# Two attention blocks on one core: the late tiles of A projected in pairs for each load of weights, with the loads of weights and of k moved to other steps

## The chip, the core and the metric

The kernel runs on one core of a Trainium2 chip. Its engines are TensorE (PE, with PEld for its weight loads), VectorE (DVE), ScalarE (ACT), GpSimd (POOL) and SyncE (SP), whose queue issues nearly all DMAs here. The metric is the device time of one execution in microseconds, less being better; a version's time is the median of several executions.

## What is computed

Two independent multi-head attentions over 2048 rows of 640 numbers in fp32, 32 heads of 20, each with its own input and weights. A is local and dilated (each row looks at eight rows, two apart, backwards), B is full attention. The outputs stand side by side.

```python
def _A_ref(x, wqkv, wo):          # H = 32, Dh = 20, W, dil = 8, 2
    qkv = (x @ wqkv).reshape(B, S, 3, H, Dh)   # then split into q, k, v
    idx = pos[:, None] - (jnp.arange(W) * dil)[None, :]
    kg, vg = k[:, :, idx_c, :], v[:, :, idx_c, :]
    logits = jnp.where(mask, jnp.einsum("bhsd,bhswd->bhsw", q, kg) * scale, -1e9)
    o = jnp.einsum("bhsw,bhswd->bhsd", softmax(logits), vg)
    return o.reshape(B, S, D) @ wo

def _B_ref(x, wqkv, wo):
    scores = jnp.einsum("bhqd,bhkd->bhqk", q, k) * (Dh ** -0.5)
    o = jnp.einsum("bhqk,bhkd->bhqd", softmax(scores), v)
    return o.reshape(B, S, D) @ wo

jnp.concatenate([a, b], axis=-1)
```

## The kernel before

**Numbers.** fp32 operands of the projections are split into a high and a low part, and three products of them (`PASSES`) stand for one fp32 product: high by high, high by low, low by high. The scores of B use the same trick within one matmul: a head's stack of q and k holds high and low rows together (`BS` = 60 rows, `BM` = 62 with two more that carry the maximum of the row).

**Stages.** First the projections: A's tiles 0 to 11 of 128 rows (the loop over `NA` parts of the weights, with the split weights kept in DRAM in `wa_d` by `a_keep`), then B's q and k (the loop over `m`), then B's v in 32 groups (`v_group`, the stage of V groups). The attention of A itself is elementwise work on POOL (`a_attention`: 4 steps of scores and 4 of values for each tile, with k and v rows fetched from `ka_d` and `va_d` into the tile `akv`), and runs beside everything else.

**The loop.** From about 397 us on, a loop of 514 steps does B's attention: 8 groups of four heads (g), 4 blocks of 512 queries (qc), 16 blocks of 128 keys (kb). Sixteen steps are a unit: one group with one query block. There are 32 units, numbered 0 to 31 here; unit 4g is the first of group g, so the first units of groups are even ones. In each step the scores of one key block are made and their exponential taken (ACT `e`), the row maxima of a unit 24 steps ahead are found (DVE `mx`), and an earlier block of exponentials is multiplied with v (`b_pv`, into an accumulator in PSUM). `UNIT_V` and `UNIT` write out the order of these on PE by hand; `b_units` plays it. A `V` in the list, near the start of each of units 0 to 23, is one call of `a_more`: it projects one of A's late tiles (12 to 15) by one of six parts m of A's weights (320 columns), 15 matmuls with the tile `wx`, in all 4 tiles by 6 parts.

**The end of a unit.** For every second key block ACT copies the accumulator out: the first copy of a unit goes to a tile `braw` (of which there are two), the later seven to tiles `more`, and POOL adds those to `braw`. At the unit's last block `normalize` starts a chain that lies in the next unit: the sums of the rows leave for DRAM (`s_d<-braw`), come back with another layout (`sm<-s_d`), DVE takes their reciprocals at the place marked `G`, these go out (`s_d<-sm`) and return spread over partitions (`rb<-s_d`), POOL multiplies `braw` by them, and four DMAs store the result (`ot_b<-braw`). The `braw` of unit u is thus free again only when its four stores have been made, in unit u+1; the first copy of unit u+2 goes to the same tile. That copy is the unit border that the text uses: "unit 10" begins when ACT starts the copy to its `braw`.

**Loads that the change touches.**

- `a_load` allocates `wx` (one buffer, shared with an earlier tile) and loads the weights of the next call in two DMAs of 800 KB (high and low part). It is called 10 steps after each `V`, and its DMAs are issued one and two steps later: 24 loads, one for each `V`.
- `b_keys(g + 1)` loads the next group's stack of k (tile `bk`) in four DMAs, two of 40 rows and two of 22. It runs at step 4 of a group; the DMAs follow 1, 2, 17 and 18 steps later, that is in steps 5 and 6 of unit 4g and in steps 5 and 6 of unit 4g+1.
- `a_columns(t)` loads the columns of A's input for tile t (320 KB) and splits them on POOL five steps later (4 operations); it runs in the stage of V groups for tile 12 and after the last `V` of a tile for the next one.
- `v_piece` loads rows of B's v for a group.

**What sets the order.** `after(n, fn)` puts a call n steps later; each engine runs its instructions in the order in which the program emits them, SP's DMA issues included. A DMA whose tile is still read, or whose source is not yet written, holds back every DMA behind it on SP. In odd units the finished tile of A is turned as well: `tr_d<-turn` and four `back<-tr_d` move 320 KB out and back.

All work on tiles goes through one line of the class `InOrder`, so the profile gives line 61 to almost everything; the tiles tell the groups apart.

Of the kernel before, what the change touches and what calls it, by code (L numbers as in the profile page):

```python
# [9 lines left out]
F32 = mybir.dt.float32  # L10
# [31 lines left out]
UP = 12  # L42
# [23 lines left out]
def attention_pair(ctx, tc, xa, wqk_a, wv_a, wo_a, xb, wqk_b, wv_b, wo_b, oa, ob):  # L66
# [6 lines left out]
    pe, gp, sp = (InOrder(tc, e) for e in (nc.tensor, nc.gpsimd, nc.sync))  # L73
# [6 lines left out]
    def after(n, fn, *args):  # L80
        due.setdefault(now[0] + n, []).append((fn, args))
# [22 lines left out]
    def tick():  # L104
        now[0] += 1
        for fn, args in due.pop(now[0], ()):
            fn(*args)
# [58 lines left out]
    wa_d = dr.tile([6, 128, 2, KC, 320], F32, name="wa_d")  # L166
# [22 lines left out]
    def big(home, shape, name):  # L189

        return sb.tile(shape, F32R, tag=f"big{home}", bufs=1, name=name)
# [6 lines left out]
    def chunk(t, xi, k):  # L198
        return t[k // (KC - 1)][:, xi, k % (KC - 1)]

    def x_pieces(x, n, second=None, at=()):

        t = columns(*at or (n,))
        src = x[:, n * 512:(n + 1) * 512].rearrange("(k p) c -> p k c", p=128)

        def piece(a, b):
            u = t[a // (KC - 1)]
            m = a % (KC - 1)
            split(u[:, 0, m:m + b - a], u[:, 1, m:m + b - a], src[:, a:b], "p", second)
        return t, [lambda a=a, b=b: piece(a, b) for a, b in PAIRS]  # L210
# [10 lines left out]
    AK = ((0, 3), (3, KC))  # L221
# [94 lines left out]
    t, more = x_pieces(xa, 1, at=(2,))  # L316
# [5 lines left out]
    t, loads = x_pieces(xa, 2, at=(3,))  # L322
# [218 lines left out]
    for n in range(NA):  # L541
        nxt = None
        for t in range(UP):
# [19 lines left out]
            if n == 1 and t == 7:  # L563
                w, more = x_pieces(xb, 0)
                XB.append(w)
                loads += more
            if n == NA - 1:
                if t in (1, 2):
                    w, more = m_pieces(MS[t - 1])
                    WB.append(w)  # L570
                    more[0]()
                if t % 4 == 0 and t:
                    w, more = x_pieces(xb, t // 4)
# [5 lines left out]
    w, loads = x_pieces(xb, 3)  # L579
# [21 lines left out]
    def v_piece(g, b0, b1):  # L601

        sp.dma_start(stacks[g][1][:, b0:b1], vb_d[b0 * 128:b1 * 128, g * GH * VC:g * GH * VC + VG]
                     .rearrange("(b p) c -> p b c", p=128))
# [7 lines left out]
    groups = 0  # L612
    for m in range(0, 10, 2):
        nxt = []
        for n in range(4):
            for j in range(2):
# [14 lines left out]
                if m < 8 and (n, j) in ((1, 0), (1, 1)):  # L631
                    w, loads = m_pieces(MS[m + 2 + len(nxt)])
# [317 lines left out]
    groups = 0  # L950

    def v_group(n, half, s):
        p = bank()
        rows15(p, lambda xi, k: chunk(XB[n], xi, k)[:, s % 4 * 128:s % 4 * 128 + 128], WV[half])
        ve = ones[s % 4]
        act.copy(ve[:, :16 * VC].rearrange("p (h c) -> p h c", c=VC)[:, :, :DH],
                 p[:, :320].rearrange("p (h d) -> p h d", d=DH))
        give(p)
        c = 16 * VC + 11 * half
        after(1, sp.dma_start, vb_d[s * 128:(s + 1) * 128, half * 16 * VC:half * 16 * VC + c], ve[:, :c])  # L960
# [7 lines left out]
            W.append(w)  # L968
            loads.extend(more)

    rows_a = [(t, m) for t in range(UP, NT) for m in range(6)]
    xt, wt = [], []
    in_dram = [UP]

    def a_columns(t):

        u = sb.tile([128, 640], F32, tag="stg", bufs=3, name="stg")
        raw = u.rearrange("p (k c) -> p k c", c=128)
        sp.dma_start(raw, xa[:, t * 128:(t + 1) * 128].rearrange("(k p) c -> p k c", p=128))
        x = (sb.tile([128, 2, KC - 1, 128], F32R, tag="last1", bufs=2, name="xn"),  # L980
             sb.tile([128, 2, 1, 128], F32R, tag="x5", bufs=2, name="xl"))

        def parts():
            for u, r in zip(x, (raw[:, :KC - 1], raw[:, KC - 1:])):
                gp.tensor_copy(u[:, 0], r)
                gp.tensor_tensor(u[:, 1], r, u[:, 0].bitcast(F32), ALU.subtract)
            xt.append(x)
        after(5, parts)

    def a_load():  # L990

        if not rows_a:
            return
        t, m = rows_a[0]
        w = big(2, [128, 2, KC, 320], "wx")
        for wi in range(2):
            after(1 + wi, sp.dma_start, w[:, wi].bitcast(F32), wa_d[m, :, wi])
        wt.append(w)

    def a_more():  # L1000

        t, m = rows_a.pop(0)
        if m == 0 and len(xt) > 1:
            xt.pop(0)
        x, w = xt[0], wt.pop(0)
        p = bank()
        rows15(p, lambda xi, k: chunk(x, xi, k), [w[:, 0], w[:, 1]])
        hf, r0 = divmod(t * 128, HS)
        pad = PAD if m > 1 else 0
        store_rows(p, (qa_d, ka_d, va_d)[m // 2][hf, pad + r0:pad + r0 + 128, m % 2 * 320:m % 2 * 320 + 320])  # L1010
        if m == 5:
            after(2, in_dram.__setitem__, 0, t + 1)
            if rows_a:
                after(2, a_columns, t + 1)
        after(10, a_load)

    V_GROUPS = [(n, half, s) for n in (2, 3, 0, 1) for half in range(2) for s in range(4 * n, 4 * n + 4)]
    v_late = V_GROUPS[-LAG:]
    for n, half, s in V_GROUPS[:-LAG]:
        v_group(n, half, s)  # L1020
        tick()
        groups += 1
        if q_loads:
            for _ in range(4 if groups == 1 else 1):
                q_loads.pop(0)()
        if groups == 1:
            wait[0] = 5
        if groups in (8, 16):
            XB[groups // 8 - 1], more = x_pieces(xb, groups // 8 - 1, gp, (groups // 8 - 1, groups // 8 + 1))
            for fn in more:  # L1030
                fn()
        if groups > 6:
            for i in islice(steps, 1):
                b_max(i)
        if groups in (9, 11, 15, 17, 19, 23, 25, 28):
            next(a_work, None)
        if groups in (26, 28):
            v_piece(0, *((0, 4) if groups == 26 else (8, 16)))
        if groups in (24, 28):
            (a_load if groups == 28 else lambda: a_columns(UP))()  # L1040
        if groups == 14:
            a_turn(*done_a.pop(0)[1:])
        turn_parts()
        if groups == 28:
            wait[0] = 2
            load_out(wo_a, WO, (0,))
        if loads and groups >= 28:
            loads.pop(0)()
# [22 lines left out]
    def flush():  # L1071
        while beside:
            op = beside.pop(0)
            (small if len(op) > 1 else op[0])(*(op if len(op) > 1 else ()))
# [9 lines left out]
    for i in range(NS + LAG):  # L1084
        g, sub = divmod(i, NQC * NKB)
        if sub == 4 and g + 1 < NG:
            for n, fn in enumerate(b_keys(g + 1)):
                after((1, 2, 17, 18)[n], fn)
            after(33, v_piece, g + 1, 0, NKB)
        if i >= NKB and i % NKB in (1, 3, 5, 7) and i // NKB + 3 < NG * NQC:  # L1090
            b_queries(*divmod(i // NKB + 3, NQC))[i % NKB // 2]()
        if i in (NS - 56, NS - 40):
            out_first((i - NS + 56) // NKB)
        tick()
        if loads and i % 2:
            loads.pop(0)()
        if i > 14 and i % 4 == 3 and next(a_work, 0) == 0:
            for d in done_a:
                d[0] -= 1
        if i % NKB == SLOT and done_a and done_a[0][0] <= 0:  # L1100
            beside.append((lambda d=done_a.pop(0): a_turn(*d[1:]),))
        turn_parts()
        if i == 1:
            load_out(wo_a, WO, (1,))

            spare += [sb.tile([128, 2, 512], F32, tag="last0", bufs=2, name="more") for _ in range(2)]
        if i < NS - LEAD:
            next(steps, None)
            if not left_a[0] and not WO_b:
                load_out(wo_b, WO_b)  # L1110
            continue
        read_at.clear()
        flush()
        if i < NS:
            b_qk(i)
        if i % 2:
            b_pv(i - LAG - 1)
            b_pv(i - LAG)
            if fill:
                fill.pop(0)()  # L1120
# [57 lines left out]
```

## Time and profile before

| what | value |
|---|---|
| time, median of 3 runs (lowest to highest) | 1801.79 us (1799.25 to 1805.84) |
| the profiled execution: its own time, and the span of its instructions | 1804.91 us, 1803.1 us |
| PE busy | 1766.3 us, 98% |
| DVE, ACT, POOL busy | 1345.8 us (75%), 1333.3 us (74%), 1230.8 us (68%) |
| DMA traffic | 289.41 MB, 161 GB/s on average |
| stage of projections of A, and of q and k of B | 0 to 318 us |
| stage of V groups | 318 to 397 us |
| units 0 to 23 of the loop (with a `V` each) | 400.57 to 1431.48 us |
| the rest of the loop and the output projection of B | 1431.48 us to the end |

The span runs from the first to the last instruction; the execution's own time is 1.8 us more. A row of a group reads: line, engine, operation, out<-in by the program's names, sizes, count, then the time busy. In a view of waits each row is "who waited <- for whom: us in total, times, longest". In a timeline each row is start, duration, engine, operation, tiles, count, and in brackets how long the engine sat idle before it and what ended that. SPq rows are issues of DMAs by SP, not the transfers. The windows view gives, for a stretch, its length, each engine's busy time (and count of instructions), then the granted share of the TensorE clock, the mean busy share of the 16 DMA engines, and GB/s.

### The profile page before, as it was taken

Reading aid. Unit: us, or ns where it says so; the run is one execution under the profiler, and the core shown is the slowest. Engines: PE = TensorE matmul, PEld = TensorE weight load, DVE = VectorE, ACT = ScalarE, POOL = GpSimd, SP = SyncE. Lnnn points to the kernel's source line nnn. Section 1 sums busy time; section 2 is a strip of 40 time slices with the busy share of each in tenths; the row PEclk is TensorE's granted clock in tenths of the full one; section 3 lists DMA queues with packets and bytes.
Section 4 is the critical chain, followed back from the end, with each engine's and each line's share of the span. In section 5 each row is a group of like instructions: output and inputs, shape, how many; then the busy total and the mean of one; then the engine's idle time right before and its main releaser. Section 6 shows DMA issues by size and latency. Waiting matters only on the chain.

```text
span 1803.1 us, 32021 instructions
## 1 busy us (share of the span) xinstructions
PE 1766.3 (98%) x11331; PEld 1010.4 (56%) x11331; DVE 1345.8 (75%) x1819; ACT 1333.3 (74%) x2598; POOL 1230.8 (68%) x1088
## 2 busy tenths in 40 slices
PE   9999999999999999999999999999999999999999
PEld 7988888774444445444444444444544444444569
DVE  3102232779899989998999899989889999999400
ACT  4323222239799989998989898888889999989981
POOL 0000782686788888897989798979787988845532
PEclk9999999999999999999999999999999999999999
DMA  7657877865545553555465546554554534222223
GB/s 255 192 178 247 296 255 244 243 201 144 154 148 154 170 163 125 173 152 165 155 167 164 181 136 188 161 161 139 169 164 143 139 111 123 80 69 66 63 70 113
DMA packets 212137, 289.41 MB, mean 161 GB/s; under 512 B 91660, under 2 KB 131724, under 8 KB 210984
## 3 DMA queue, kind: packets, MB, share of 16 engines
q1 hardware_dynamic: 211400, 286.70, 52.0%
q8 instruction: 89, 1.46, 0.3%
q14 instruction: 72, 0.59, 0.1%
q10 hardware_dynamic: 576, 0.66, 0.1%
HBM read 212.53 MB, written 74.74 MB: 159 GB/s over the span
## 4 chain that ended last, share of the span: by engine, by line
PE 85%; DVE 6%; DMA 6%; ACT 1%; issue 1%; SPq 0%; POOL 0%; ACTq 0%; DVEq 0%
PE ps_st L61 85%; DVE mx L61 6%; DMA ot_b<-braw 3%; DMA wx<-wa_d 2%; ACT e L61 1%; DMA bq<-qb_d 1%; DMA stg<-wv_b 0%; ACT braw L61 0%; DMA stg<-xa 0%; SPq L61 0%; DMA qb_d<-pr 0%; POOL am L61 0%; DVE xl L61 0%; ACTq L61 0%; DVE pr L61 0%
## 5 line engine op out<-in xcount | busy, mean ns | idle before, releaser
L61 DVE TENSOR_REDUCE mx<-ps_st 128x1 f32<-128x512 f32 (+1 forms) x1500 | 1220.0, 878 | 116.1 <-PE ps_st L61 105.9
L61 ACT ACTIVATE e<-ps_st 128x512 f32<-128x512 f32 x2048 | 1067.2, 608 | 38.2 <-PE ps_st L61 19.1
L61 PE MATMUL ps_st<-bq,bk 62*128 62x512 f32 x2048 | 611.9, 442 | 0.8 <-DVE mx L61 0.6
L61 PE MATMUL ps_st<-bk,bq 60*128 60x512 f32 x2048 | 559.0, 434 | 26.0 <-ACT braw L61 23.7
L61 PEld LDWEIGHTS ps_st<-bq,bk 62*128 62x128 f32 x2048 | 289.7, 185 | 479.8 <-ACT e L61 352.9
L61 PE MATMUL ps_st<-e,vb 128*32 128x512 f32 x4096 | 542.9, 604 | 3.2 <-ACT e L61 0.3
L61 POOL TENSOR_TENSOR braw<-braw,more 128x512 f32<-128x512 f32 x224 | 288.2, 1287 | 220.7 <-ACT more L61 200.4
L61 POOL TENSOR_TENSOR akv<-akv,aq 128x1280 f32<-128x1280 f32 x64 | 188.6, 2947 | 184.4 <-DVE w L61 184.4
L61 PEld LDWEIGHTS ps_st<-bk,bq 60*128 60x128 f32 x2048 | 270.5, 185 | 60.9 <-ACT braw L61 27.2
L61 POOL TENSOR_TENSOR akv<-akv 128x640 f32<-128x640 f32 (+3 forms) x304 | 282.9, 930 | 23.8
L61 ACT COPY ro<-ps_st 128x320 f32<-128x320 f32 (+2 forms) x132 | 62.5, 475 | 201.6 <-PE ps_st L61 169.0
L61 PEld LDWEIGHTS ps_st<-e,vb 128*32 128x32 f32 x4096 | 82.0, 108 | 158.6 <-issue 72.0
L61 POOL TENSOR_TENSOR akv<-akv,al 128x1280 f32<-128x1280 f32 x64 | 152.1, 2377 | 0.2
L61 ACT COPY more<-ps_st 128x512 f32<-128x512 f32 x224 | 132.5, 592 | 1.9 <-PE ps_st L61 1.4
L61 PE MATMUL ps_st<-ww,xn 128*128 128x320 f32 x768 | 125.8, 314 | 0.0
L61 PEld LDWEIGHTS ps_st<-ww,xn 128*128 128x128 f32 x768 | 113.6, 188 | 19.9 <-ACT e L61 8.4
L61 PE MATMUL ps_st<-xn,w 128*128 128x512 f32 x480 | 117.6, 393 | 0.0
L61 PEld LDWEIGHTS ps_st<-xn,w 128*128 128x128 f32 x480 | 90.1, 188 | 21.0
L61 PE MATMUL ps_st<-wc,xn 128*128 128x512 f32 (+1 forms) x432 | 101.5, 380 | 0.1
L61 ACT CAST pr<-ps_st 128x512 fp32r<-128x512 f32 x40 | 23.5, 589 | 103.5 <-PE ps_st L61 103.5
L61 DVE TENSOR_TENSOR pr<-ps_st,pr 128x512 fp32r<-128x512 f32 x40 | 27.7, 691 | 92.9 <-ACT pr L61 90.1
L61 PEld LDWEIGHTS ps_st<-wc,xn 128*128 128x128 f32 x432 | 79.9, 188 | 14.5 <-ACT xn L61 0.8
(69 smaller groups left out, 1083.8 us busy)
## 6 DMA issues: line engine op xcount, KB each, us to landing
akv<-ka_d SPq DMA_DIRECT2D x128, 320.0 KB
akv<-va_d SPq DMA_DIRECT2D x128, 320.0 KB
wx<-wa_d SPq DMA_DIRECT2D x48, 800.0 KB
kb_d<-pr SPq DMA_DIRECT2D x20, 512.0 KB
qb_d<-pr SPq DMA_DIRECT2D x20, 512.0 KB
bk<-kb_d SPq DMA_DIRECT2D x16, 640.0 KB
bq<-qb_d SPq DMA_DIRECT2D x64, 160.0 KB
rb<-s_d SPq DMA_DIRECT2D x128, 64.0 KB
```

Source lines behind the costliest of these rows:

```text
L61: return self.tc.keep_in_program_order(op(*a, **k))
```

## The change

Four edits:

1. The 24 calls of `a_more` run in another order: tiles 12 and 13 take turns on each part m, then 14 and 15. One load of `wx` serves two calls, so there are 12 loads in place of 24. A load is issued in four DMAs (the 3 and 2 chunks of rows `AK` of the high part, then of the low part; 480 and 320 KB), 2 to 5 steps after the second of the two calls, which lands in steps 5 to 8 of odd units. The first load moves from V groups 29 and 30 to groups 25 to 28.
2. The four DMAs of the next k stack go in steps 5 to 8 of unit 4g, all of them.
3. The columns of tiles 12 and 13 are both loaded in the stage of V groups (after groups 18 and 21), those of 14 and 15 twelve steps after the last call of tile 12 and of tile 13 (units 10 and 11).
4. In the stage of V groups two pieces of v (`v_piece`, blocks 8 to 16) are loaded earlier, after groups 22 and 23 in place of 28.

```diff
-    rows_a = [(t, m) for t in range(UP, NT) for m in range(6)]
-    xt, wt = [], []
+    rows_a = [(t + j, m) for t in range(UP, NT, 2) for m in range(6) for j in range(2)]
+    xt, wt = {}, []
...
     def a_load():
 
-        if not rows_a:
-            return
-        t, m = rows_a[0]
         w = big(2, [128, 2, KC, 320], "wx")
-        for wi in range(2):
-            after(1 + wi, sp.dma_start, w[:, wi].bitcast(F32), wa_d[m, :, wi])
-        wt.append(w)
+        wt[:] = [w]
+        m = rows_a[0][1]
+        return [lambda wi=wi, a=a, b=b: sp.dma_start(w[:, wi, a:b].bitcast(F32), wa_d[m, :, wi, a:b])
+                for wi in range(2) for a, b in AK]
 
     def a_more():
 
         t, m = rows_a.pop(0)
-        if m == 0 and len(xt) > 1:
-            xt.pop(0)
-        x, w = xt[0], wt.pop(0)
+        x, w = xt[t], wt[0]
...
         if m == 5:
             after(2, in_dram.__setitem__, 0, t + 1)
-            if rows_a:
-                after(2, a_columns, t + 1)
-        after(10, a_load)
+            if t + 2 < NT:
+                after(12, a_columns, t + 2)
+        if t % 2 and rows_a:
+            for n, fn in enumerate(a_load()):
+                after(2 + n, fn)
...
-        if groups in (26, 28):
-            v_piece(0, *((0, 4) if groups == 26 else (8, 16)))
-        if groups in (24, 28):
-            (a_load if groups == 28 else lambda: a_columns(UP))()
+        if groups in (22, 23, 26):
+            v_piece(0, *((8, 12), (12, 16), (0, 4))[(groups - 21) // 2])
+        if groups in (18, 21):
+            a_columns(UP + groups // 21)
+        if groups == 24:
+            for n, fn in enumerate(a_load()):
+                after(1 + n, fn)
...
             for n, fn in enumerate(b_keys(g + 1)):
-                after((1, 2, 17, 18)[n], fn)
+                after(1 + n, fn)
```

PE, ACT and DVE run the same operations in the same order as before; SP and POOL do not. On SP, in the second half of an odd unit (unit 3), where the turned tile comes back and `braw` is stored, these rows stand before the change:

```order
L61 DMA back<-tr_d 32x20x32 x4
L61 DMA wx<-wa_d 128x1600 x2
L61 DMA akv<-va_d 128x640 x2
L61 DMA bq<-qb_d 20x1024
L61 DMA ot_b<-braw 20x512 x4
L61 DMA bq<-qb_d 40x1024
```

And the same place after it:

```order
L61 DMA back<-tr_d 32x20x32 x4
L61 DMA akv<-va_d 128x640 x2
L61 DMA bq<-qb_d 20x1024
L61 DMA ot_b<-braw 20x512 x4
L61 DMA bq<-qb_d 40x1024
```

The two loads of `wx` ahead of the four stores of `braw` are gone there, and in the even units too. In the first half of the same odd unit SP has now, between the return of the sums and the store of their reciprocals:

```order
L61 DMA sm<-s_d 128x16
L61 DMA wx<-wa_d 128x960
L61 DMA wx<-wa_d 128x640
L61 DMA bq<-qb_d 40x1024
L61 DMA wx<-wa_d 128x960
L61 DMA akv<-va_d 128x640 x2
L61 DMA wx<-wa_d 128x640
L61 DMA oa<-ro 128x320
L61 DMA s_d<-sm 128x16
```

All four pieces stand behind `sm<-s_d` and ahead of `oa<-ro`, the first DMA of the second half. In unit 4, the first of a group, SP has before the change:

```order
L61 DMA bk<-kb_d 40x4096
L61 DMA bq<-qb_d 20x1024
L61 DMA sm<-s_d 128x16
L61 DMA bk<-kb_d 22x4096
L61 DMA bq<-qb_d 40x1024
L61 DMA aq<-qa_d 128x640
L61 DMA akv<-ka_d 128x640 x2
```

And after it:

```order
L61 DMA bk<-kb_d 40x4096
L61 DMA bq<-qb_d 20x1024
L61 DMA sm<-s_d 128x16
L61 DMA bk<-kb_d 22x4096
L61 DMA bk<-kb_d 40x4096
L61 DMA bq<-qb_d 40x1024
L61 DMA bk<-kb_d 22x4096
L61 DMA aq<-qa_d 128x640
L61 DMA akv<-ka_d 128x640 x2
```

The second half of the k stack has come here from steps 5 and 6 of the next unit by the program's count of steps, which SP had issued at the end of this unit and the start of the next.

More of the change, by code (lines that the diff above doesn't have):

```diff
@@ L986, in parts @@
                 gp.tensor_tensor(u[:, 1], r, u[:, 0].bitcast(F32), ALU.subtract)
-            xt.append(x)
+            xt[t] = x
         after(5, parts)
     def a_load():
-        if not rows_a:
-            return
-        t, m = rows_a[0]
         w = big(2, [128, 2, KC, 320], "wx")
-        for wi in range(2):
-            after(1 + wi, sp.dma_start, w[:, wi].bitcast(F32), wa_d[m, :, wi])
-        wt.append(w)
+        wt[:] = [w]
+        m = rows_a[0][1]
+        return [lambda wi=wi, a=a, b=b: sp.dma_start(w[:, wi, a:b].bitcast(F32), wa_d[m, :, wi, a:b])
+                for wi in range(2) for a, b in AK]
     def a_more():
         t, m = rows_a.pop(0)
-        if m == 0 and len(xt) > 1:
-            xt.pop(0)
-        x, w = xt[0], wt.pop(0)
+        x, w = xt[t], wt[0]
         p = bank()
```

## Prediction

> **What bounds the kernel now.** I read the page first, then the waits of each engine within the loop, then the timeline around the longest of them, then windows over single units.
>
> ```profile
> span 1803.1 us, 32021 instructions
> PE 85%; DVE 6%; DMA 6%; ACT 1%; issue 1%; SPq 0%; POOL 0%; ACTq 0%; DVEq 0%
> core 0: 1803.1 us, clock 0.991
> ```
>
> The chain that ended last is PE for 85% of the span; 6% of it runs over DMAs. Where does PE wait in the loop? The waits from 397 to 1700 us, ACT's own three and PE's largest:
>
> ```profile
> ACT braw L61 <- DMA ot_b<-braw: 24.8, 8, 4.1
> ACT braw L61 <- PE ps_st L61: 1.7, 2, 0.9
> ACT braw L61 <- DVE mx L61: 1.7, 1, 1.7
> PE ps_st L61 <- ACT braw L61: 23.7, 11, 3.7
> ```
>
> PE has one wait worth the name, on ACT's copy to `braw`: 11 times, 23.7 us. ACT in turn waits 8 times for the stores of the `braw` of two units ago, 24.8 us, the longest 4.1. The other three (1.7 and 1.7 us) I put to the same cause, since the same copy waits for the same semaphores and the view names only the last one. So 28.2 us of waits on one tile. One of the eight, from unit 9 to unit 10, on SP:
>
> ```profile
> 790.04 0.34 SPq L61 DMA_DIRECT2D sm<-s_d  x1
> 790.84 0.82 SPq L61 DMA_DIRECT2D akv<-va_d  x2
> ...
> 805.52 0.47 SPq L61 DMA_DIRECT2D s_d<-sm  x1
> ...
> 814.95 2.69 SPq L61 DMA_DIRECT2D back<-tr_d  x4
> 817.74 1.29 SPq L61 DMA_DIRECT2D wx<-wa_d  x2
> 819.09 1.12 SPq L61 DMA_DIRECT2D akv<-va_d  x2
> ...
> 820.76 2.11 SPq L61 DMA_DIRECT2D ot_b<-braw  x4
> ```
>
> and on POOL, ACT and PE:
>
> ```profile
> 813.19 1.29 POOL L61 TENSOR_TENSOR braw<-braw,rb 128x512 f32<-128x512 f32 x1
> 828.72 0.59 ACT L61 COPY braw<-ps_st 128x512 f32<-128x512 f32 x1 [2.98 <-DMA ot_b<-braw]
> 829.35 0.50 PE L61 MATMUL ps_st<-bk,bq 60*128 60x512 f32 x1 [2.58 <-ACT braw L61]
> ```
>
> `braw` is ready at 814.5 (813.19 + 1.29), but its stores are issued from 820.76 on, behind `back`, the two `wx` loads of 800 KB and an `akv`, and they land just before 828.7. ACT stands 2.98 us, PE 2.58. What a unit costs with and without this, in windows from copy to copy (units 0 to 23 together, then 7, 8, 9, 10 and 23):
>
> ```profile
> 400.57:1431.48 1030.91, 1002.55 (x6866) 483.17 (x6867) 949.48 (x1307) 913.05 (x1789) 856.62 (x753) 0.99 0.52 156
> 701.26:743.25 41.99, 41.88 (x293) 20.19 (x293) 40.70 (x59) 37.98 (x76) 38.46 (x34) 1.00 0.45 138
> 743.25:784.62 41.37, 40.68 (x282) 19.23 (x283) 38.40 (x52) 38.15 (x75) 33.18 (x30) 1.00 0.60 185
> 784.62:828.72 44.10, 42.04 (x293) 20.18 (x293) 42.67 (x61) 37.95 (x76) 40.47 (x36) 1.00 0.55 153
> 828.72:871.45 42.73, 41.90 (x281) 20.53 (x283) 36.53 (x49) 38.14 (x75) 31.15 (x28) 0.96 0.51 164
> 1389.96:1431.48 41.52, 41.39 (x288) 19.49 (x289) 39.80 (x58) 37.98 (x75) 38.03 (x34) 1.00 0.40 111
> ```
>
> Unit 9 ends with the wait: 44.10 − 2.98 = 41.12 without it. Unit 10 has none, yet takes 42.73 where unit 8 takes 41.37: the last columns but two show why, its granted clock is 0.96. A wait of this length costs a second time, 1.36 us, as a spell of lower clock just after it. In unit 10 the spell is (1 − 0.96) × 42.73 × 2 = 3.4 us at half clock, and the mean clock of 0.991 over the span is 0.009 × 1803.1 × 2 = 32 us at half, nine such spells, near the eight long waits. The Trainium skill, "TensorE: Matmul & The Clock Gate", section "HAM oscillation — how this bites in real kernels", has the rule that a gap of PE beyond some 3.4 us drops it to half clock and that half of the throttled time is lost. The trace shows the drop after 2.58 us already, and the price per spell is 1.36 us by rows, 1.7 by the page; over 32 us that would be 12.8 or 16 us.
>
> **The change part by part.**
>
> *The loads of weights leave the end of the units.* Traffic first, from the list of DMA issues and from windows:
>
> ```profile
> wx<-wa_d SPq DMA_DIRECT2D x48, 800.0 KB
> bk<-kb_d SPq DMA_DIRECT2D x16, 640.0 KB
> 790.60:797.00 6.40, 6.40 (x48) 2.69 (x47) 6.40 (x8) 6.18 (x13) 4.39 (x4) 1.00 0.90 176
> 797.00:805.00 8.00, 7.93 (x57) 4.83 (x53) 7.67 (x18) 7.23 (x15) 7.39 (x11) 1.00 0.03 11
> 814.00:828.70 14.70, 12.77 (x91) 5.08 (x89) 14.40 (x18) 11.42 (x23) 14.39 (x11) 1.00 0.91 285
> 747.80:756.00 8.20, 8.17 (x61) 3.42 (x60) 8.06 (x11) 7.99 (x17) 4.15 (x3) 1.00 0.83 197
> 756.00:764.30 8.30, 8.14 (x57) 4.74 (x54) 7.32 (x13) 7.46 (x15) 6.44 (x8) 1.00 0.34 99
> ```
>
> In the last 14.7 us of unit 9 the DMA engines are 91% busy at 285 GB/s; from 797 to 805 they are 3% busy. The change takes 1.64 MB out of the first stretch, 1.64 MB / 285 GB/s = 5.7 us of its work, and 1.29 us of SP's issuing, and half of all such loads vanish. What the stores gain is bounded by 1.3 us (the issue alone) below and 5.7 us above. I take the upper end, for two reasons. The waits of SP from 784 to 829 us say that its later issues hang on the loads too:
>
> ```profile
> SPq L61 <- DMA wx<-wa_d: 2.6, 2, 1.8
> SPq L61 <- DMA s_d<-sm: 2.8, 1, 2.8
> ```
>
> (2.6 us that go, whereas the 2.8 us for the reciprocals stay). And unit 23 is already what an odd unit will be: it has `back`, `akv` and the stores, but no load of weights behind its `V`:
>
> ```profile
> 1418.72 2.70 SPq L61 DMA_DIRECT2D back<-tr_d  x4
> ...
> 1424.03 1.44 SPq L61 DMA_DIRECT2D ot_b<-braw  x4
> ```
>
> Its stores are issued 34.1 us after its start (unit 9: 36.1), all four within 1.44 us (unit 9: 2.11), and the copy at 1431.48 starts without idle time. A gain of 5.7 us covers the longest wait of 4.1.
>
> The sum, two ways. By waits: 28.2 us, and 9.4 spells × 1.36 = 12.8; together 41.0. By units: if all 24 ran like unit 8, 24 × 41.37 = 992.9 against 1030.91, 38.0 us. Unit 23 (41.52) is a little above that, unit 9 without its wait (41.12) a little below. I take **38.0**, which leaves room for small waits under 1 us like that at the end of unit 7; 41 stays as the end of the range below.
>
> *The loads in steps 5 to 8 of odd units.* The four pieces follow `sm<-s_d` (790.04 in unit 9). With the `akv` of 0.66 MB that is 2.3 MB from about 791; at 176 to 285 GB/s it ends at 799 to 804, inside the idle stretch and ahead of `s_d<-sm` at 805.52. What is queued behind them on SP: `bq`, which is for a unit three later, `akv`, and then nothing for 14 us. The `akv` issued at 790.84 is used here:
>
> ```profile
> 815.68 2.37 POOL L61 TENSOR_TENSOR akv<-akv,al 128x1280 f32<-128x1280 f32 x1
> ```
>
> 24.8 us later, so 8 us of delay cost nothing. The next `V` reads the weights a unit later. Cost 0; if that cover were gone, POOL would be late by what `akv` is late, and `braw` with it.
>
> *The k stack in one piece.* The first halves of the stack in unit 8 and what follows:
>
> ```profile
> 747.76 0.31 SPq L61 DMA_DIRECT2D bk<-kb_d  x1
> ...
> 764.21 0.38 SPq L61 DMA_DIRECT2D s_d<-sm  x1
> ...
> 777.19 1.45 SPq L61 DMA_DIRECT2D ot_b<-braw  x4
> ```
>
> The 756 to 764 window is 34% busy: the second half (0.99 MB, 5.0 us at the 197 GB/s beside it) fits, and ends about when `s_d<-sm` starts. If it overlaps, the reciprocals come up to 2 us later, in a unit that has no `back`, loses 5.7 us of weights and had no wait at its end. Cost 0, bounds −1 (the start of unit 4g+1 is freed) to +2 us once per group.
>
> *Columns and v.* The columns of tiles 14 and 15 (320 KB, 1.1 us at 285 GB/s) now stand ahead of the stores in units 10 and 11, and those of two other units go; POOL's four operations each are as many as before. Bounds −2 to +2 us; I take 0. In the stage of V groups the loads come some four groups earlier, and PE's waits there are on no DMA; 0, with up to 4 us (one wait of 2.6 and its spell) if a store of v is held back.
>
> Sum for the profiled execution: 1804.9 − 38.0 = 1766.9. It stands 3.1 us above the median of the runs, so for a median I predict 1801.8 − 38.0 = **1764 us**.
>
> **The rivals.**
>
> *Only the issue is saved.* `back` and `akv` stay ahead of the stores, and the transfers may be so spread over the DMA engines that the stores land only 1.3 us earlier. Then 24.8 − 8 × 1.3 = 14.4 us of waits stay with most spells; gained are 10.4 + 3.4 = 13.8, which gives 1788. For it: unit 9's reciprocals came back 2.8 us late and that stays. Against: unit 23. Chance 0.10.
>
> *It does not do what it says:* `back` alone decides, the weights only filled time in which the stores waited anyway, and nothing that can be measured moves: 1799. Against it stands the same unit, and that even units, without `back`, show no wait at all speaks for it. Chance 0.07.
>
> *A new wait, and slower.* DVE takes the reciprocals of the sums in its fixed place:
>
> ```profile
> 803.36 0.20 DVE L61 RECIPROCAL sm<-sm 128x16 f32<-128x16 f32 x1
> DVE sm L61 <- DMA sm<-s_d: 14.1, 2, 7.1
> ```
>
> In unit 9 that is 13.3 us after `sm<-s_d` was issued; at the end of the kernel DVE did wait for it twice, 7.1 us at most. In the first unit of a group it stands behind 640 KB of k with 1.4 MB following. If the small transfer landed later than those 13 us, DVE and then PE would stand: 7 groups × (7.1 + 1.36) = 59 us, and 1764 + 59 = 1823. Against: a whole half stack and its neighbours were done by about 760, 12 us after issue, with the small one ahead of half of it. Chance 0.06.
>
> **How the numbers follow.** Forecast 0.77, the rivals 0.10, 0.07 and 0.06. The forecast's own range is 1764 − 3 (the sum by waits) − 4 (the bounds of the k stack, the columns, and a run's scatter) to 1764 + 8 (the upper bounds of stack, columns and V groups), 1757 to 1772. To hold the time 8 times in 10 it takes in half of the first rival: 1756 to 1783. A measurement of this kernel tells 0.5%, 9 us, from no change. Faster by more: forecast and first rival, 0.87; within: 0.07; slower: 0.06.
>
> **What would show it.** Right: ACT's waits for `ot_b<-braw` gone or under 3 us in all, clock 1.00 in the windows of all units, units 0 to 23 in some 993 us, DMA busy in the first half of odd units and below 70% in the last 14 us. Wrong: waits of 2 us or more left at the ends of units 1, 5, 9 and so on (first rival), ACT's wait unchanged (second), DVE waiting for `sm<-s_d` within the loop (third), or PE waiting on `wx`.

## The result, and the profile after

| | median of the runs (lowest to highest) | profiled execution | clock |
|---|---|---|---|
| before | 1800.52 us (1798.07 to 1805.84, 4 runs) | 1804.91 us | 0.991 |
| after | 1771.25 us (1770.04 to 1776.2, 4 runs) | 1771.62 us | 0.999 |

The ratio is 0.9839, with a 95% interval of 0.9809 to 0.9868: the change saves 29.3 us by the medians and 33.3 us between the two profiled executions. The forecast was 1764 us; the time is 7.3 us above it, within the range. First the page of the kernel after: its span, the chain that ended last, and its DMA packets.

```profile
span 1769.8 us, 31997 instructions
PE 85%; DMA 4%; DVE 4%; POOL 3%; issue 1%; SPq 1%; ACT 1%; DVEq 0%; POOLq 0%; ACTq 0%
DMA packets 212152, 269.74 MB, mean 152 GB/s; under 512 B 91676, under 2 KB 131740, under 8 KB 211000
```

DMA's share of the chain has gone from 6% to 4%, and the traffic from 289.41 to 269.74 MB, which are the twelve loads of 1.64 MB that pairing saves. The waits in units 0 to 23 (400 to 1398 us), first ACT's largest, then PE's largest:

```profile
ACT ro L61 <- PE ps_st L61: 53.1, 48, 1.6
...
PE ps_st L61 <- DMA bq<-mdr: 3.9, 5, 1.1
```

No row of ACT's copy to `braw` is left, where there were 28.2 us, and PE no longer waits for that copy. In its place stands a row that the kernel before did not have: PE waits five times for the rows with the maxima (`bq<-mdr`). The windows from copy to copy say what the two are worth: units 0 to 23 together, then units 4, 6 and 9, then the last 14.2 us of unit 9.

```profile
403.34:1397.50 994.16, 985.55 (x6866) 470.15 (x6867) 948.93 (x1307) 912.76 (x1789) 854.38 (x750) 1.00 0.49 142
568.25:610.74 42.49, 41.15 (x288) 19.46 (x290) 39.38 (x53) 38.18 (x76) 32.92 (x27) 1.00 0.55 149
651.83:693.20 41.37, 41.13 (x288) 19.69 (x290) 39.25 (x53) 38.16 (x76) 34.01 (x30) 1.00 0.40 121
776.15:817.27 41.12, 41.01 (x288) 19.67 (x289) 39.84 (x58) 37.93 (x75) 38.70 (x37) 1.00 0.51 150
803.10:817.30 14.20, 14.20 (x104) 5.68 (x104) 14.04 (x19) 13.88 (x28) 13.96 (x12) 1.00 0.74 211
```

Units 0 to 23 take 994.16 us, 36.7 less than before, at a clock of 1.00. Odd units (41.12) and most even ones (41.37) run as the wait-free units of before did. Unit 4, the first of a group, takes 42.49. In unit 9 the end is busy still, 74% of the DMA engines at 211 GB/s (before: 91% at 285). What SP issues in unit 9, and the copy that ends it:

```profile
781.49 0.85 SPq L61 DMA_DIRECT2D wx<-wa_d  x2
...
806.60 2.70 SPq L61 DMA_DIRECT2D back<-tr_d  x4
809.34 1.12 SPq L61 DMA_DIRECT2D akv<-va_d  x2
...
811.30 1.40 SPq L61 DMA_DIRECT2D ot_b<-braw  x4
...
817.27 0.59 ACT L61 COPY braw<-ps_st 128x512 f32<-128x512 f32 x1
```

The stores are issued 35.2 us after the start of the unit (before: 820.76 − 784.62 = 36.1). The issue has come only 1 us earlier, and still the copy, which stood 2.98 us before, has no idle time in front of it. The rest lies between issue and transfer. In the packets of the traces (2 KB each, one row of a store) the first row follows the issue by 4.9 us before and by 1.7 after, and the last one ends 43.1 and 39.2 us after the start of the unit. What the stores gained is the 1.6 MB that no longer go ahead of them.

**Where 33.3 us come from.** Units 0 to 23: −36.7. The first copy to `braw` comes at 403.34 in place of 400.57: +2.8. The rest of the span, 1803.1 − 1431.48 = 371.6 before and 1769.8 − 1397.5 = 372.3 after: +0.7, which is within what this stretch varies by in the other profiles (371.5 to 372.4). So something went wrong in two places, and both are one kind of wait.

*The k stack.* Unit 4 on SP, then POOL's product and PE's wait:

```profile
572.76 0.31 SPq L61 DMA_DIRECT2D bk<-kb_d  x1
...
573.95 1.05 SPq L61 DMA_DIRECT2D bk<-kb_d  x2
575.66 0.35 SPq L61 DMA_DIRECT2D bk<-kb_d  x1
...
589.20 0.38 SPq L61 DMA_DIRECT2D s_d<-sm  x1
...
594.76 2.15 SPq L61 DMA_DIRECT2D rb<-s_d  x4
597.03 1.74 SPq L61 DMA_DIRECT2D mdr<-mtr  x4
...
600.13 0.56 SPq L61 DMA_DIRECT2D bq<-mdr  x2
```

```profile
598.64 1.28 POOL L61 TENSOR_TENSOR braw<-braw,rb 128x512 f32<-128x512 f32 x1 [2.68 <-DMA rb<-s_d]
603.02 0.50 PE L61 MATMUL ps_st<-bq,bk 62*128 62x512 f32 x1 [1.10 <-DMA bq<-mdr]
```

The 8 KB of reciprocals (`s_d<-sm`) are issued at 589.20, 20.9 us into the unit, and `rb<-s_d`, which must wait for their landing, only at 594.76, 5.6 us later (in units 4 and 8 of the kernel before it came some 1.5 us later). SP stands in between, and what stands behind it on SP is `mdr<-mtr` and `bq<-mdr`, which have nothing to do with the reciprocals: they bring the maxima for the next scores on PE. Why the 8 KB landed late is seen in the DMA view's row of busy shares. Its 40 slices run from 744 to 765 us of the kernel before (unit 8) and from 572 to 592 us of the kernel after (unit 4):

```profile
DMA  8200000099163896969997977766662000000007
```

```profile
DMA  0069125687676985956999988662789586247566
```

Before, the DMA engines fall idle at about 760, five microseconds ahead of the next store. After, they are busy right to the end of the stretch, and `s_d<-sm` goes out into it.

*The stage of V groups.* ACT and PE after:

```profile
386.78 0.43 ACT L61 COPY ve<-ps_st 128x320 f32<-128x320 f32 x1 [3.57 <-DMA vb_d<-ve]
390.71 0.42 ACT L61 COPY ve<-ps_st 128x320 f32<-128x320 f32 x1 [3.50 <-DMA vb_d<-ve]
391.40 0.46 PE L61 MATMUL ps_st<-bq,bk 62*128 62x512 f32 x1 [1.92 <-DMA bq<-mdr]
```

Before, PE's longest idle time between 380 and 402 us was 0.86. Now the first load of weights and two pieces of v stand there ahead of small DMAs, and PE waits 1.92 us. (ACT is idle some 2.6 us before most copies of this stage in any case, waiting for PE, so about 0.9 us of each of its two waits is new.) The only spell of lower clock of this execution, but for its last 1.4 us, follows: 3.41 us at half from 392.89 on.

### The profile page after: what moved, and what is told of

It is laid out like the page before. It is cut to its first block, busy times and chain, and to the rows that moved or that the text cites. A ratio compares the mean times of both kernels' runs of the same rounds, so it can differ in the third digit from the quotient of the medians.

```text
span 1769.8 us, 31997 instructions
## 1 busy us (share of the span) xinstructions
PE 1751.3 (99%) x11331; PEld 999.9 (56%) x11331; DVE 1345.4 (76%) x1819; ACT 1333.0 (75%) x2598; POOL 1230.0 (70%) x1088
## 2 busy tenths in 40 slices
DMA packets 212152, 269.74 MB, mean 152 GB/s; under 512 B 91676, under 2 KB 131740, under 8 KB 211000
## 4 chain that ended last, share of the span: by engine, by line
PE 85%; DMA 4%; DVE 4%; POOL 3%; issue 1%; SPq 1%; ACT 1%; DVEq 0%; POOLq 0%; ACTq 0%
PE ps_st L61 85%; DVE mx L61 4%; DMA s_d<-sm 1%; POOL akv L61 1%; SPq L61 1%; DMA bq<-mdr 1%; ACT e L61 1%; DMA bq<-qb_d 1%; POOL xn L61 0%; DMA stg<-wv_b 0%; DMA mdr<-mtr 0%; DMA wx<-wa_d 0%; DMA qb_d<-pr 0%; POOL xl L61 0%; POOL ao L61 0%
## 5 line engine op out<-in xcount | busy, mean ns | idle before, releaser
L61 PEld LDWEIGHTS ps_st<-xn,w 128*128 128x128 f32 x480 | 90.2, 188 | 20.9
L61 ACT CAST pr<-ps_st 128x512 fp32r<-128x512 f32 x40 | 23.5, 587 | 103.6 <-PE ps_st L61 103.6
```

Of the source, the lines that this page charges most:

```text
L61: return self.tc.keep_in_program_order(op(*a, **k))
```

## The experiments

**Theories.** (P) *Place*: the bytes of the weights ahead of the four stores at the end of the odd units made all the waits; moving them is the whole gain. (T) *Traffic*: half the loads is what counts, wherever they lie. (I) *Issue*: SP's time for the two DMAs counts, not the bytes. For the 4 to 6 us given back: (K) the k stack in one piece, and (F) the early first load in the stage of V groups.

### Place and traffic apart

Place alone: the kernel before, with all 24 loads, each in the four pieces right after its `V`.

```diff
-        for wi in range(2):
-            after(1 + wi, sp.dma_start, w[:, wi].bitcast(F32), wa_d[m, :, wi])
+        for n, (wi, (a, b)) in enumerate((wi, ab) for wi in range(2) for ab in AK):
+            after(lag + n, sp.dma_start, w[:, wi, a:b].bitcast(F32), wa_d[m, :, wi, a:b])
...
-        after(10, a_load)
+        a_load()
```

> The kernel before, with one thing of the change: each of its 24 loads of weights goes in four pieces 2 to 5 steps after its call, in steps 5 to 8 of every unit. No pairs, k and the stage of V groups as before. Theory (the place ahead of the stores of braw is what cost the time): ACT waits for ot_b<-braw under 3 us in all, no spell of lower clock, units 0 to 23 in 990 to 997 us, time 1762 to 1770. Rival (half the traffic is what counts): the traffic is that of before, so the waits stay above 12 us and the time above 1785. Second rival (two loads in steps 5 to 8 of a group's first unit, weights and k together, jam there): waits on bq<-mdr in units 4, 8, 12 and so on.

Pairs alone: the kernel after with 12 loads, each of two DMAs and in the old place; the k stack, the first load and the pieces of v as before, too.

```diff
-            for n, fn in enumerate(a_load()):
-                after(2 + n, fn)
+            after(10, a_load)
...
-                after(1 + n, fn)
+                after((1, 2, 17, 18)[n], fn)
```

> The changed kernel with its loads of weights back where they were in odd units: two pieces of 800 KB, 11 and 12 steps after the second call of a pair; k in steps 5, 6, 21, 22 as before; first load and v pieces in the stage of V groups as before, but both columns early (after groups 18 and 21). Half of the traffic of the weights, none of the new places. Theory (place): the eight long waits all follow odd units, and these keep their loads, so ACT's waits for ot_b<-braw stay at 20 to 28 us and the time at 1790 to 1803. Rival (traffic): waits fall to about half, 10 to 14 us, time 1783 to 1789. For the stage of V groups: if the early columns on POOL are what made PE wait 1.92 us for bq<-mdr at 391 us, the first copy to braw stays at 403 us; if the early weights are, it comes at 400.5 to 401.

| | median (lowest to highest) | ratio to before (95%) |
|---|---|---|
| place alone | 1765.45 us (1765.22 to 1766.17) | 0.9809 (0.9783 to 0.9835) |
| pairs alone | 1800.34 us (1797.11 to 1803.82) | 1.0004 (0.9989 to 1.002) |

Units 0 to 23 in place alone, in the windows view (PE's only wait from 397 to 1440 us is one of 0.3):

```profile
400.98:1391.98 991.00, 986.23 (x6866) 471.24 (x6866) 948.70 (x1307) 913.04 (x1790) 856.53 (x753) 1.00 0.57 163
```

and in pairs alone, the window, ACT's waits on the copy and PE's:

```profile
403.11:1428.16 1025.05, 1001.60 (x6866) 482.37 (x6866) 949.33 (x1307) 912.89 (x1790) 854.87 (x752) 0.99 0.48 138
```

```profile
ACT braw L61 <- DMA ot_b<-braw: 18.9, 8, 3.5
ACT braw L61 <- POOL akv L61: 2.8, 1, 2.8
ACT braw L61 <- DVE mx L61: 1.1, 1, 1.1
ACT braw L61 <- PE ps_st L61: 0.7, 1, 0.7
...
PE ps_st L61 <- ACT braw L61: 19.0, 11, 3.0
```

Place alone moves 163 GB/s in these units, more than any kernel here without added copies, and has no wait on the copy. Pairs alone moves 138 and keeps 23.5 of the 28.2 us. The place is the whole gain; halving the traffic is worth nothing in this kernel, since the twelve loads that it saves lay in units that had no wait at their end. (Nor is it worth anything where no wait is left: pairs at the new place, with the stack of k and the first load put back, take 1765.84 us below.) And place alone is 5.8 us faster than the change (6.2 us when both ran again on one chip, at 1767.19, 1765.44 to 1768.35, and 1773.35, 1771.27 to 1778.07, with no overlap):

> place_alone once more beside the changed kernel. If the place is the whole gain and the rest of the change costs: 1765 to 1767, 4 to 7 us below changed_again. If chips differ by as much: within 2 us of it.

> The changed kernel itself, on the same chip as the others of this call. If its new waits (k stack, stage of V groups) are a matter of place and not of the execution: again 1770 to 1774, five waits on bq<-mdr in the first units of groups, and one on bq<-mdr before the first copy to braw.

One reading of pairs alone misled: its first copy to `braw` is as late as in the kernel after (403.11), which looks like the loss in the stage of V groups. It isn't. PE's wait for `bq<-mdr` is gone there, and what is late is the start of the stage, by a wait of 1.51 us on `bq<-qb_d` at 318.02 (before: 0.51 at 316.95) and a spell of lower clock right behind it. The time of one event sums all that lies before it; the stage by itself, from the ninth V group's copy to the first copy to `braw`, takes 76.4 us in pairs alone, 76.5 before and 78.6 after.

### Bytes or issue: a dose at the old place

Place alone plus copies of a part of `wa_d` into a DRAM tile that nothing reads, issued where the loads of the odd units stood. Nothing that is computed changes; the copies are added work. The doses are two DMAs of 1.3 KB (the issue only), 480 + 320 KB, and 2 × 800 KB.

```diff
+    def again(m):
+        for wi, part in enumerate(((slice(0, 128), slice(0, 3)), (slice(0, 128), slice(0, 2)))):
+            after(1 + wi, sp.dma_start, junk[wi, part[0], part[1]], wa_d[m, part[0], wi, part[1]])
...
         a_load()
+        calls[0] += 1
+        if calls[0] % 2 == 0:
+            after(10, again, m)
```

> place_alone with two DMAs of 1.3 KB each added in odd units where the loads stood before (11 and 12 steps after the V): SP's two issues without the bytes. It prices the lower bound of the prediction. Theory (bytes ahead of the stores cost the time): no waits on ot_b<-braw above 1 us in all, 1765 to 1767. Rival (SP's issuing and the order of its queue cost it): waits of 8 us or more in all, 1773 or above.

> As dose_issue, with 480 and 320 KB copied within DRAM in place of the small ones: half the bytes of the old loads. Theory: the stores land some 2.9 us later; the margin at the ends of the odd units after a group's first unit is 5.7 less 3.1 to 4.1 us, so only these six show waits, of about 1 us, 4 to 8 us in all, one or no spell of low clock: 1768 to 1775. Rival (all or nothing): as with no bytes, or as with all.

> As dose_issue, with 800 KB twice: all bytes of the old loads, on top of the loads at their new place. Theory: the eight long waits return, 20 to 30 us in all, with their spells of low clock, 1795 to 1805: as before, with more traffic. Rival (it was not the bytes, but that the next load had to be there): the time stays below 1775.

| dose | median (lowest to highest) | ratio to before (95%) | clock |
|---|---|---|---|
| issue only | 1767.36 us (1766.56 to 1768.97) | 0.9813 (0.9786 to 0.984) | 0.999 |
| half the bytes | 1776.9 us (1775.4 to 1777.89) | 0.9864 (0.9837 to 0.9891) | 0.998 |
| all the bytes | 1817.2 us (1808.17 to 1822.49) | 1.0094 (1.0073 to 1.0114) | 0.991 |

ACT's waits on the copy, for the three doses in this order:

```profile
ACT braw L61 <- DMA ot_b<-braw: 1.5, 1, 1.5
ACT braw L61 <- PE ps_st L61: 0.7, 1, 0.7
```

```profile
ACT braw L61 <- DMA ot_b<-braw: 6.8, 4, 2.3
ACT braw L61 <- DVE mx L61: 1.8, 1, 1.8
ACT braw L61 <- DMA bq<-qb_d: 1.0, 1, 1.0
ACT braw L61 <- DMA akv<-va_d: 1.0, 1, 1.0
```

```profile
ACT braw L61 <- DMA ot_b<-braw: 14.9, 6, 4.4
ACT braw L61 <- DMA bq<-qb_d: 7.1, 2, 3.6
ACT braw L61 <- DVE mx L61: 4.1, 2, 3.0
ACT braw L61 <- POOL akv L61: 3.5, 1, 3.5
ACT braw L61 <- POOL braw L61: 2.0, 1, 2.0
```

The sums are 2.2, 10.6 and 31.6 us. The issue brings back next to nothing; the bytes bring back all, and the spells of lower clock with them (0.999, 0.998, 0.991). So I falls. The time does not grow in proportion: half the bytes cost some 10 us over the issue alone, all of them 50. What does grow with each dose is the time from the issue of the stores to their first packet, by the median of the odd units 1 to 21: 2.0 us in place alone, then 2.2, 3.4 and 5.4 with the three doses, and 4.8 in the kernel before. It fits that the slack at the end of a unit absorbs the first part, and that what goes past it is waited for and draws spells too; the slack was not measured by itself. Nor was it tried whether the stores stand in line behind the bytes or share the engines with them. Both larger doses came out above what was expected of them; the copies go from DRAM to DRAM, which the old loads into SBUF did not, so the times show the direction and not the size. (The profile of the full dose was taken in its fastest run, 1808.17.)

### What was given back

The kernel after with the k stack in two halves again:

```diff
-                after(1 + n, fn)
+                after((1, 2, 17, 18)[n], fn)
```

> The changed kernel with the k stack back in steps 5, 6, 21 and 22. Theory (the stack in one piece made s_d<-sm late, SP held mdr behind rb, PE waited for bq<-mdr): PE's five waits on bq<-mdr in units 4, 8, 12, 16, 20 (3.9 us) go, these units fall from 41.9 to 42.5 to 41.4, units 0 to 23 in 989 to 991 us, time 4 us below the changed kernel, 1767. Rival (the second half of the stack at the end of those units and the start of the next delays the stores of braw): ACT's waits for ot_b<-braw come back in units 5, 9, 13 or at their ends, at 1 us or more each, and the time is not below the changed kernel's.

It took 1767.55 us (1766.39 to 1768.07; ratio 0.9819, 0.9788 to 0.985), 3.7 us less than the change. Units 0 to 23:

```profile
402.94:1393.69 990.75, 985.55 (x6866) 470.76 (x6866) 948.52 (x1307) 912.70 (x1790) 857.20 (x753) 1.00 0.50 143
```

994.16 − 990.75 = 3.4 us in the loop, and of PE's waits for `bq<-mdr` there one of 0.5 is left. SP's waits for the reciprocals' store from 400 to 1432 us say the same at the source: before, after, and with the two halves.

```profile
SPq L61 <- DMA s_d<-sm: 37.0, 23, 3.6
```

```profile
SPq L61 <- DMA s_d<-sm: 56.0, 24, 5.1
```

```profile
SPq L61 <- DMA s_d<-sm: 37.4, 24, 3.3
```

Next, the stack in one piece but two steps earlier:

```diff
-        if sub == 4 and g + 1 < NG:
+        if sub == 2 and g + 1 < NG:
...
-            after(33, v_piece, g + 1, 0, NKB)
+            after(35, v_piece, g + 1, 0, NKB)
```

> The changed kernel with the k stack, still in one piece, in steps 3 to 6 of a group's first unit in place of 5 to 8 (and v two steps later by its own count, so in its old step). In the changed kernel the stack's transfers ran to 21 or 22 us after the unit's start and s_d<-sm was issued at 20.9. Theory (the end of the stack holds s_d<-sm, that holds rb, and rb holds mdr and bq<-mdr on SP): the stack ends some 5 us earlier, rb is issued 22.5 to 24 us after the start in place of 26.5, PE's waits on bq<-mdr in units 4, 8, 12, 16, 20 fall below 1 us in all, units 0 to 23 in 990 to 991.5 us, 1768 to 1769. Rival (the stack in one piece is slow in itself, since its rows of 16 KB keep few DMA engines busy, and anything beside it waits): rb stays at 25 us or later and the time at 1771.

It took 1767.83 us (1766.2 to 1770.74; ratio 0.9811, 0.9796 to 0.9825), 5.5 us less than the change run beside it on the same chip (1773.35), and units 0 to 23 took 990.13. In units 4, 8, 12, 16 and 20 `rb<-s_d` is issued 22.5 to 23.6 us after the start, in the kernel after 25.5 to 26.5. So it is not the one piece as such that costs, but that it is still running when the small store goes out. K stands.

Then the two halves, and the first load and the pieces of v in their old places as well:

```diff
-        if groups in (22, 23, 26):
-            v_piece(0, *((8, 12), (12, 16), (0, 4))[(groups - 21) // 2])
+        if groups in (26, 28):
+            v_piece(0, *((0, 4) if groups == 26 else (8, 16)))
...
-        if groups == 24:
+        if groups == 28:
             for n, fn in enumerate(a_load()):
```

> The changed kernel with the k stack in steps 5, 6, 21, 22 (as in k_as_before) and, in the stage of V groups, the first load of weights after groups 29 to 32 and the v pieces as in the kernel before; the early columns stay. Theory (the early weights, not the columns on POOL, held the stores of v and bq<-mdr back in that stage): no wait of ACT on vb_d<-ve and none of PE on bq<-mdr there, 2 us below k_as_before, 1765 to 1766, and so no better than place_alone (1765.45) although it moves half of the weights. Rival (the columns): the wait of 1.5 to 1.9 us stays, 1767.5. Rival (half the traffic is worth something once no wait is left): below 1763.

It took 1765.84 us (1765.05 to 1766.99; ratio 0.9804, 0.9781 to 0.9826), 1.7 us under the one with the stack alone put back. The medians are from two sets of runs and their ratios overlap, so what counts is the stage: from the ninth V group's copy on it takes 76.4 us in place of 78.2. ACT there still waits once, for the store of `ve`, but PE's wait for `bq<-mdr` is gone (0.34 us is its longest idle time from 380 to 402):

```profile
388.24 0.42 ACT L61 COPY ve<-ps_st 128x320 f32<-128x320 f32 x1 [3.09 <-DMA vb_d<-ve]
```

The first copy to `braw` comes at 400.02 in place of 402.94, of which some 1.1 us is an earlier start of the stage. F stands, though the edit moves the load and the two pieces of v together: which of the two holds the store back was not tried.

Last, the loads of the kernel after in two DMAs of 800 KB at the same steps:

```diff
-        return [lambda wi=wi, a=a, b=b: sp.dma_start(w[:, wi, a:b].bitcast(F32), wa_d[m, :, wi, a:b])
-                for wi in range(2) for a, b in AK]
+        return [lambda wi=wi: sp.dma_start(w[:, wi].bitcast(F32), wa_d[m, :, wi]) for wi in range(2)]
```

> The changed kernel with each load of weights in two DMAs of 800 KB, in steps 5 and 6 of odd units, in place of four. Theory: the stretch has idle DMA time behind it, so nothing changes, 1771 within 3 us, units 0 to 23 in 993 to 996 us. Rival (the pieces matter, since a large DMA holds up the small sm<-s_d and akv beside it): waits on sm<-s_d or akv appear in odd units and the time is 5 us or more above.

It took 1773.93 us (1772.77 to 1776.1; ratio 0.9857, 0.983 to 0.9884). That is 2.7 us above the change, but only 0.6 above its second set of runs (1773.35), and within the 3 us that had been expected: no loss is shown. What its profile has more lies in the same two places, PE's waits in the loop, and the one in the stage of V groups:

```profile
PE ps_st L61 <- DMA bq<-mdr: 4.8, 5, 1.7
```

```profile
393.06 0.76 PE L61 MATMUL ps_st<-bq,bk 62*128 62x512 f32 x1 [3.28 <-DMA bq<-mdr]
```

The stage takes 80.0 us, against 78.6 and 78.8 in two executions of the kernel after. The loop's five waits fall in first units of groups, where no load of weights is issued, and run from 0.6 to 1.7 us; another run of the unchanged kernel after had 4.6 us in four such waits with a longest of 2.0, so the loop's part is scatter between executions. The stage's part would fit larger pieces ahead of a small store; one profile doesn't show it.

## Why the prediction was right, and where it was off

1. *One cause for ACT's 28.2 us of waits, the three odd rows included.* Right. All rows vanish with the place of the loads, and in the dose runs the same copy shows `bq<-qb_d`, `mx`, `akv` as the named releaser of waits that the bytes alone bring back.
2. *The spells of lower clock go with them (12.8 us).* Right: clock 1.00 in units 0 to 23, and the spells come back with the dose. (In the clock records of before they are seven, two of them of double length: nine times 3.41 us.)
3. *The relief of the stores lies between 1.3 us (issue) and 5.7 (bytes), taken at 5.7.* Right, and for the reason given: in unit 9 the issue came 1.0 us earlier and the last row of the stores 3.9; over the odd units 1 to 21 that is 3.3 to 6.7, 5.0 in the median, near the upper bound. The issue alone as a dose costs 2.2 us of waits where the bytes cost 31.6. The first rival (1788) falls by it, the second (no change) by the result itself. One sign was missed: the end of odd units is 74% busy, not below 70%, and it doesn't matter.
4. *The sum over units, 38.0, with 41 by the waits as its end.* The removed waits and spells are worth 40: 1030.91 − 990.75 with the stack in two halves, 1030.91 − 991.00 in place alone. So 41 by the waits was the better of the two sums, and unit 8 was a good pattern that lay 0.1 us high. That the change got 36.7 is the next point.
5. *The k stack in one piece costs 0 (−1 to +2 us once per group).* This is the step that failed. The working said that the second half takes 5.0 us "and ends about when `s_d<-sm` starts", and in the bounds took a late reciprocal for the concern of the stores of `braw`. Both halves were off. The 5.0 us came from 197 GB/s, which was the rate of all transfers in that window and not the stack's: in the packets of unit 8 (16 KB each, one row of the stack) the first half alone runs from 748.7 to 756.8, 8.1 us, and in unit 4 of the kernel after the whole stack from 573.7 to 591.2. So the stack was still running 20.9 us into the unit, the store landed late (5.6 us between its issue and that of `rb`, in unit 4), and the one who paid was not the end of the unit but whatever SP had queued behind `rb<-s_d`, `mdr` and `bq<-mdr`, and so PE in the same unit. Its size, 3.4 us in the loop, is within the bounds of a group (0.7 on average in each of five), and those are units 4, 8, 12, 16 and 20. The third rival had the place (first units of groups) and the direction, but named the wrong queue: DVE's reciprocals were not late, SP's issue behind them was.
6. *The stage of V groups costs 0, "with up to 4 us (one wait of 2.6 and its spell) if a store of v is held back".* The bound happened: ACT waits 3.57 and 3.50 us for stores of v, PE 1.92, one spell follows, and the first copy comes 2.8 us late, of which 0.6 is a later start of the stage. About +2.2.
7. *Loads in steps 5 to 8, and the columns, cost 0.* Right. Place alone has such loads in odd and even units and shows no wait on them. In the kernel after the columns are loaded in units 10 and 11, and these take 41.39 and 41.10 us, as much as units without them. (Two of the runs with pairs have a wait of PE on `bq<-mdr` in unit 9, 0.5 and 0.8 us; the cause was not looked for.)

The profiled execution adds up: 1804.9 − 36.7 + 2.8 + 0.7 = 1771.7, and it took 1771.62. The forecast for it was 1766.9, 4.7 us less: 3.4 us for the stack of k, 2.8 and 0.7, together 6.9 us that the sum had put at nothing, less the 2.2 by which 40.2 exceeds its 38.0. That these partly cancel is luck. The other 2.6 us of the 7.3 come from the last step, in which 38.0 was taken off a median that is 3.1 us below the profiled execution. Those 3.1 us most likely were part of the waits themselves: the runs of before scatter over 7.8 us, those of place alone over 0.95, and in both kernels without them, after and place alone, the profiled time and the median agree within 0.4. What is saved from a long-waiting execution isn't saved again from a typical one. That is argued from the scatter, not tried by itself.

## What to carry to other kernels

- When a large transfer moves, look for the small DMAs after its new place whose landing something waits for, and follow that queue: the cost appears at whatever is issued behind the waiting one, here PE's maxima behind the reciprocals on SP.
- Ask of bytes *where* before *how many*: the same bytes some 25 us earlier in the unit were free, and leaving half of them out, with the other half in the old place, saved nothing. Here the plain move without pairing is the fastest kernel of all, 1.9% under the kernel before, and the change with its k stack and first load put back equals it.
- Where the scatter of the runs lies in the waits that a change removes, take the saving off the execution that it was read from.

## What was not expected of the hardware

**The clock.** A short idle time of PE decides over 1.4 us of clock, and it need not be 3 us long. In unit 4 PE waited 2.00 us (601.69 to 603.69) in the second run of the change, and 1.69 us (603.64 to 605.33) in the kernel with two pieces. The windows around the first wait, then those around the second:

```profile
600.62:604.03 3.41, 1.41 (x12) 0.85 (x8) 2.35 (x3) 2.42 (x6) 3.33 (x2) 1.00 0.93 308
604.03:607.45 3.42, 3.42 (x16) 1.03 (x14) 1.25 (x2) 1.19 (x2) 3.11 (x6) 0.50 0.74 216
```

```profile
601.05:604.46 3.41, 2.59 (x20) 1.06 (x16) 3.39 (x5) 3.30 (x9) 3.41 (x3) 1.00 0.72 222
604.46:607.87 3.41, 2.54 (x20) 0.99 (x24) 1.70 (x3) 1.70 (x5) 3.25 (x3) 1.00 0.79 268
607.87:611.29 3.42, 3.38 (x26) 1.17 (x20) 3.35 (x5) 3.42 (x8) 3.11 (x6) 1.00 0.68 216
```

After the first wait the clock is 0.50 for one window, and that unit took 44.9 us where the other execution of the same kernel took 42.5. After the second it stays at 1.00. The edges of these windows come from the traces' clock records: in all 13 profiles each spell, but for the one at the very end, begins a whole number of 3.41 us after the first record and lasts one or two times 3.41 us. By the rows, what decides is how long PE is idle inside one such slot, and not how long one wait is: the 2.00 us fell into one slot, the 1.69 us across the edge of two. Counted over all slots of the 13 profiles that ran at full clock, each of the 28 with 1.5 us or more of idle PE was followed by half clock, two of seven with 1.2 to 1.4 us were, and none with less. The 1.52 us of the kernel with the stack in two halves, in the stage of V groups, lay in one slot and were followed by a spell. The Trainium skill, "TensorE: Matmul & The Clock Gate", section "HAM oscillation — how this bites in real kernels", puts the limit at gaps of some 3.4 us. These rows disagree: 1.5 us inside one slot is enough.

**The stack of k is slow for its bytes.** Its 1.98 MB were still being moved more than 16 us after the first issue, beside 1.3 MB of others: 3.33 MB in the 20 us of the DMA view above, 167 GB/s, where all transfers at the end of unit 9 of before, the weights among them, went at 285. The Trainium skill, "DMA: Bandwidth & Descriptors", section "Why a DMA increments its semaphore by 16 and not by 1", says that a DMA uses the largest number of engines up to 16 that divides its slowest dimension; by an estimate from that, 40 and 22 rows would get 10 and 11. That fits the direction, but no view shown here has the engines one by one, and a stack of other row counts was not run. The Trainium skill, the same page, section "Bandwidth", advises to batch transfers to 1 MiB or more. No run here has a load of that size; between pieces of 480 and 320 KB and of 800 no difference is shown (1771.25 and 1773.35 against 1773.93 us).
